# Attention to a few agents ahead of a cosine feed-forward layer: the places of side work move from steps 1, 3 and 5 of a chunk to 2, 4 and 6

## The chip, the cores and the metric

The kernel runs on one core of a Trainium2 chip. The metric is the device time of one execution in microseconds; the lower, the better. The engines are TensorE (PE; its weight loads are listed apart as PEld), VectorE (DVE), ScalarE (ACT), GpSimd (POOL) and SyncE (SP), whose queue issues the DMAs.

## What is computed

Four batches of 12,480 tokens of 128 channels attend to 49 agents: the agents gather values over all keys, each query gathers from the agents, and every token then goes through a feed-forward layer of 2,048 hidden columns with g = h cos(h). All arrays are float32.

```python
def sm(a, b):
    s = scale * (a @ b.transpose(0, 2, 1))
    s = s - s.max(-1, keepdims=True)
    e = np.exp(s)
    return e / (e.sum(-1, keepdims=True) + 1e-09)
a2k = sm(agents, k)
agent_v = a2k @ v
q2a = sm(q, agents)
x = (q2a @ agent_v).reshape(B * N, C)
h = x @ w_in
return (h * np.cos(h)) @ w_out
```

## The kernel before

The agents' values times w_in are one small matrix `a` of 49 rows (held twice) by 2,048 per batch, so a token's hidden columns come straight from its 49 weights: h = a^T pT. A query group of 960 tokens (13 groups a batch, 52 in all) is two chunks of 480 columns; a chunk is NP = 8 steps of two blocks of 128 hidden columns each. The main loop counts steps n over all chunks, 16 to a group. A step issues:

- a hidden pair: two matmuls of 480 columns into a `ph` tile (L557). There are three `ph` buffers of two PSUM banks;
- its cosine on ACT (`c`, L560) and (c - 1) h on DVE (`r`, L562), which frees the `ph` buffer;
- whatever the plan holds for step n (`plan.run(n)`);
- the output pair of the step n - LAG, four steps back: two matmuls into the chunk's output `po` (L579). Step 7 of a chunk adds two more (L575, L576), and then ACT copies `po` to `osb` (L581).

`po` takes one of the two buffers of the pool `ps_1` (`one` in the profile). The side work shares the other: agent scores of the next batch (L90, copied by ACT at L173), query scores (L90, copied at L351; then the maximum on DVE at L355 and a subtraction on POOL), transposes of a group's weights (`query_turned`, L379, copied by ACT at L381; then four POOL operations that make `pT`), values (L235, added by DVE at L240), and projections to the next `a` (L266). A lot of scores, transposes or values fills one buffer of that pool until it is copied.

The plan gives each such lot a step by `extra(n, ...)`: the first step at or after n that no other lot has and whose output step (n - LAG) % 8 is allowed. `dense=True` allows more places; it is used beside a burst. A burst is a stretch on ACT with a table load, exponentials of agent scores and query scores, and a table load back to the cosine, at steps 108, 132 and 156 of a batch (output step 0), and an early one near step 18. The tile scheduler then orders each engine's instructions: it takes what is ready by its own model, in the priority of the code, so a lot may be issued ahead of the step at which the code has it.

In the profile an L90 matmul has two records, so a lot of eight has 16; an L557 or L579 matmul has one.

Of the kernel before, what the change touches and what calls it, by code (L numbers as in the profile page):

```python
# [35 lines left out]
LAG = 4  # L36
# [4 lines left out]
def agent_attention_cos_ffn(ctx, tc, qT, kT, v, agT, w_in, w_out, outT):  # L41
# [9 lines left out]
    NP = NF // 2  # L51
# [250 lines left out]
    with ExitStack() as pools:  # L302
# [152 lines left out]
        taken = set()  # L455

        def extra(n, f, *args, dense=False):


            while n in taken or (n - LAG) % NP not in ((1, 2, 3, 4, 5) if dense else (1, 3, 5)):  # L460
                n += 1
            taken.add(n)
            plan(n, f, *args)
            return n

        for n in range(1, NQ):
            plan(n * STEP - 10, query_weights, n)
            extra(n * STEP - 7, query_turned, n)

        def spread_out(todo, t, end):  # L470

            for i, lot in enumerate(todo):
                t = extra(t, *lot) + 1
                if i + 1 < len(todo):
                    t += max(0, (end - t) // (len(todo) - i - 1) - 1)
            return t
# [9 lines left out]
        def beside(at, todo):  # L486

            for lot in todo[:3]:
                extra(at, *lot, dense=True)
            return todo[3:]  # L490
# [236 lines left out]
```

## Time and profile before

| | |
|---|---|
| median of 3 runs | 1238.58 us (1237.95 to 2774.02) |
| profiled execution | 1242.72 us |
| its span, first to last instruction | 1241.0 us |
| mean granted TensorE clock | 0.971 |
| PE busy, weight loads busy | 1180.0 us (95%), 975.0 us (79%) |
| DVE busy | 1067.3 us (86%) |
| ACT busy | 982.4 us (79%) |
| POOL busy | 353.5 us (28%) |

The busy time of PE is a sum over records whose ends are modelled; the rows below give starts as well. Times in rows are from the start of the span.

### The profile page before, as it was taken

How to read it: one execution, taken by the hardware profiler on the slowest of the kernel's cores; microseconds unless marked ns; L12 is line 12 of the kernel's file. 1: busy time of each engine (PE TensorE's matmuls, PEld its weight loads, DVE VectorE, ACT ScalarE, POOL GpSimd, SP SyncE). 2: the span in 40 equal slices, each digit the busy share in tenths (PEclk: the TensorE clock that was granted, in tenths of full speed). 3: DMA queues.
4: the chain of work that ended last, by engine and by line, in shares of the span. 5: the costliest groups of instructions: out<-in, count | busy, mean ns of one | idle time of the engine just before them, and what ended most of it. 6: DMA issues, size and time to landing. Idle time of an engine off the chain costs nothing.

```text
span 1241.0 us, 17334 instructions
## 1 busy us (share of the span) xinstructions
PE 1180.0 (95%) x6349; PEld 975.0 (79%) x6349; DVE 1067.3 (86%) x1171; ACT 982.4 (79%) x1176; POOL 353.5 (28%) x389
## 2 busy tenths in 40 slices
PE   8998999899999999989999999998999999998997
PEld 8887888788887888868787888887878776776674
DVE  6797888877889988887989888887888999999997
ACT  2267788878878888778878888887887888888996
POOL 1102313433331313172332313126331323121220
PEclk9798999989999999989999999998999999998999
DMA  8782332124422233322241232332321001000000
GB/s 313 217 229 66 104 103 80 64 69 141 126 80 68 76 96 96 99 63 94 65 128 64 80 98 78 96 96 80 96 80 49 32 32 48 16 33 17 32 32 35
DMA packets 39190, 107.74 MB, mean 87 GB/s; under 512 B 4344, under 2 KB 4728, under 8 KB 39096
## 3 DMA queue, kind: packets, MB, share of 16 engines
q1 hardware_dynamic: 39096, 106.55, 27.4%
q8 instruction: 52, 0.85, 0.3%
q14 instruction: 42, 0.34, 0.1%
HBM read 80.97 MB, written 25.56 MB: 86 GB/s over the span
## 4 chain that ended last, share of the span: by engine, by line
PE 70%; DVE 12%; ACT 12%; issue 4%; DMA 0%; POOL 0%; ACTq 0%; SPq 0%; DVEq 0%
PE ph L557 25%; PE one L579 18%; PE one L90 12%; DVE r L562 9%; ACT c L560 6%; PE one L235 5%; ACT osb L581 3%; PE ph L235 3%; PE one L575 2%; PE one L576 2%; PE one L379 1%; PE ph L98 1%; ACT e L360 1%; DVE mx L355 1%; PE one L266 1%
## 5 line engine op out<-in xcount | busy, mean ns | idle before, releaser
L562 DVE SCALAR_TENSOR_TENSOR r<-c,ph 128x960 fp32r<-128x960 f32 x832 | 924.1, 1149 | 96.2 <-ACT c L560 90.4
L560 ACT ACTIVATE c<-ph 128x960 f32<-128x960 f32 x832 | 797.7, 978 | 166.4 <-PE ph L557 147.6
L557 PE MATMUL ph<-pT,a 113*128 113x480 f32 x1664 | 546.9, 410 | 16.9 <-DVE r L562 14.2
L579 PE MATMUL one<-r,w 128*128 128x480 f32 x1664 | 513.2, 390 | 1.2 <-ACT osb L581 0.7
L557 PEld LDWEIGHTS ph<-pT,a 113*128 113x128 f32 x1664 | 287.4, 192 | 114.5 <-DVE r L562 56.7
L579 PEld LDWEIGHTS one<-r,w 128*128 128x128 f32 x1664 | 310.9, 191 | 47.7 <-ACT osb L581 2.0
L90 PEld LDWEIGHTS one<-ag,xt 128*120 128x120 f32 x1408 | 180.6, 194 | 49.5 <-ACT osb L581 27.9
L90 PE MATMUL one<-ag,xt 128*120 128x49 f32 x1408 | 180.2, 273 | 21.5 <-ACT e L351 10.9
L370 POOL TENSOR_TENSOR p<-e,rz 120x392 f32<-120x392 f32 x52 | 44.3, 857 | 474.2 <-PE one L379 397.2
L385 POOL TENSOR_TENSOR pT<-p,pT 49x480 fp32r<-49x480 f32 x104 | 126.7, 1218 | 8.0
L235 PEld LDWEIGHTS one<-s,vt 120*128 120x128 f32 x624 | 77.8, 191 | 10.2 <-ACT osb L581 4.3
L357 POOL TENSOR_TENSOR e<-e,mx 120x392 f32<-120x392 f32 x49 | 41.3, 844 | 155.7 <-DVE mx L355 150.9
L384 POOL CAST pT<-p 49x480 fp32r<-49x480 f32 x104 | 60.7, 584 | 75.5 <-ACT p L381 53.0
L235 PE MATMUL one<-s,vt 120*128 120x98 f32 x624 | 79.3, 273 | 2.5 <-DVE av L240 1.1
L581 ACT COPY osb<-one 128x480 f32<-128x480 f32 x104 | 57.7, 554 | 3.0 <-PE one L579 2.9
L224 POOL TENSOR_TENSOR es<-es,s 120x392 f32<-120x392 f32 x36 | 36.7, 1020 | 46.5 <-ACT s L216 44.1
L379 PEld LDWEIGHTS one<-ident,p 120*113 120x113 f32 x208 | 31.7, 178 | 12.2 <-ACT osb L581 7.1
L575 PE MATMUL one<-pT,b 113*128 113x480 f32 x104 | 40.5, 389 | 0.0
L212 POOL TENSOR_TENSOR s<-s,mxb 120x1568 f32<-120x1568 f32 (+1 forms) x9 | 31.6, 3537 | 29.8 <-DVE mxb L208 29.8
L576 PE MATMUL one<-pT,b 113*128 113x480 f32 x104 | 39.9, 384 | 0.0
L379 PE MATMUL one<-ident,p 120*113 120x120 f32 x208 | 37.6, 274 | 2.3 <-ACT osb L581 2.3
L351 ACT COPY e<-one 120x392 f32<-120x392 f32 x49 | 23.8, 487 | 18.7 <-PE one L90 18.4
(92 smaller groups left out, 544.1 us busy)
## 6 DMA issues: line engine op xcount, KB each, us to landing
xt<-qT SPq DMA_DIRECT2D x52, 480.0 KB, 3.5
vt<-v SPq DMA_DIRECT2D x104, 240.0 KB, 3.4
outT<-osb SPq DMA_DIRECT2D x51, 480.0 KB, 2.6
xt<-kT SPq DMA_DIRECT2D x46, 480.0 KB, 3.5
c<-kT SPq DMA_DIRECT2D x6, 480.0 KB, 5.6
raw<-w_in SPq DMA_DIRECT2D x8, 256.0 KB, 4.8
raw<-w_out SPq DMA_DIRECT2D x8, 256.0 KB, 4.6
outT<-osb SPq DMA_DIRECT2D x2, 240.0 KB, 2.9
```

Of the source, the lines that this page charges most:

```text
L90: nc.tensor.matmul(ps[:, t, :], xt[:, t * TT:(t + 1) * TT], ag[:, b, :], start=True, stop=True)
L235: nc.tensor.matmul(po, vt[:, t, :], twice(e[:, t, :]), start=(t == 0 and (g == 0 or not lone)), stop=(t == GT - 1 and (g == NG - 1 or not ...
L379: nc.tensor.transpose(pt[:KR, t * TT:(t + 1) * TT], p_in[n % 2][:, t, :KR], ident[:TT, :TT])
L384: nc.gpsimd.tensor_copy(pT[own, c], p[own])
L385: nc.gpsimd.tensor_sub(pT[other, c], p[own], pT[own, c].bitcast(F32))
L557: nc.tensor.matmul(ph[:, j, :CH], ai[:, f], pTs[q % 3][:, c], start=True, stop=True)
L560: nc.scalar.activation(cos, h, AF.Sin, bias=HALF_PI, scale=1.0)
L562: nc.vector.scalar_tensor_tensor(r, cos, 1.0, h, op0=ALU.subtract, op1=ALU.mult)
L575: nc.tensor.matmul(po, b1[k], pTs[q % 3][:, c], start=False, stop=False)
L576: nc.tensor.matmul(po, b2[k], pTs[q % 3][:, c], start=False, stop=False)
L579: nc.tensor.matmul(po, w1[:, f, :], r[:, j, :], start=(f == 0), stop=(f == NF - 1))
L581: nc.scalar.copy(osb[:, c * CH:(c + 1) * CH], po)
```

## The change

The places in which `extra` may put a lot are one output step later: 2, 4 and 6 for 1, 3 and 5, and 2 to 6 for 1 to 5 beside a burst.

```diff
         def extra(n, f, *args, dense=False):


-            while n in taken or (n - LAG) % NP not in ((1, 2, 3, 4, 5) if dense else (1, 3, 5)):
+            while n in taken or (n - LAG) % NP not in ((2, 3, 4, 5, 6) if dense else (2, 4, 6)):
                 n += 1
             taken.add(n)
             plan(n, f, *args)
```

Of 202 lots 173 stand one step later in the plan. The others stand one to five steps earlier: where a lot found place 5 past or taken and went to place 1 of the next chunk, it may now find place 6 free. The early burst follows its last query lot and is at step 17 instead of 18.

PE's order in the main loop, in the first chunk of a query group, from the hidden pair (L557) ahead of the chunk's first output pair (L579). L90, eight in all, is a lot of query scores, L379 the transposes. Before:

```order
L557 MATMUL ph<-pT_87,a_80 128x480 x2
L579 MATMUL one<-r,w_68 128x480 x2
L90 MATMUL one<-ag,xt 120x49 x2
L557 MATMUL ph<-pT_87,a_80 128x480 x2
L90 MATMUL one<-ag,xt 120x49 x6
L579 MATMUL one<-r,w_68 128x480 x2
L557 MATMUL ph<-pT_87,a_80 128x480 x2
L579 MATMUL one<-r,w_68 128x480 x2
L379 MATMUL one<-ident,p_93 113x120 x3
L557 MATMUL ph<-pT_87,a_80 128x480 x2
L579 MATMUL one<-r,w_68 128x480 x2
L379 MATMUL one<-ident,p_93 113x120
```

And now, at the same place:

```order
L557 MATMUL ph<-pT_87,a_80 128x480 x2
L579 MATMUL one<-r,w_68 128x480 x2
L90 MATMUL one<-ag,xt 120x49 x3
L557 MATMUL ph<-pT_87,a_80 128x480 x2
L579 MATMUL one<-r,w_68 128x480 x2
L90 MATMUL one<-ag,xt 120x49 x3
L557 MATMUL ph<-pT_87,a_80 128x480 x2
L90 MATMUL one<-ag,xt 120x49 x2
L579 MATMUL one<-r,w_68 128x480 x2
L557 MATMUL ph<-pT_87,a_80 128x480 x2
L579 MATMUL one<-r,w_68 128x480 x2
L379 MATMUL one<-ident,p_93 113x120 x3
```

The lot begins behind the same output pair in both; its six last matmuls, which stood in one block, are now two parts with an output and a hidden pair between, and the transposes stand one step later.

ACT's order around the same place, from the copy of one finished chunk (osb) to the copy of the next but one; `e` is the query scores' copy, `p` the transposes', `s` that of agent scores. Before:

```order
L581 COPY osb<-one 128x480
L560 ACTIVATE c<-ph 128x960 x2
L351 COPY e<-one 120x392
L560 ACTIVATE c<-ph 128x960 x2
L381 COPY p<-one 113x480
L560 ACTIVATE c<-ph 128x960 x4
L581 COPY osb<-one 128x480
L560 ACTIVATE c<-ph 128x960 x2
L173 COPY s<-one 120x392
L560 ACTIVATE c<-ph 128x960 x4
L173 COPY s<-one 120x392
L560 ACTIVATE c<-ph 128x960 x2
```

And now:

```order
L581 COPY osb<-one 128x480
L560 ACTIVATE c<-ph 128x960 x3
L351 COPY e<-one 120x392
L560 ACTIVATE c<-ph 128x960 x2
L381 COPY p<-one 113x480
L560 ACTIVATE c<-ph 128x960 x3
L581 COPY osb<-one 128x480
L560 ACTIVATE c<-ph 128x960 x3
L173 COPY s<-one 120x392
L560 ACTIVATE c<-ph 128x960 x3
L173 COPY s<-one 120x392
L560 ACTIVATE c<-ph 128x960 x2
```

Three of the four copies of side work stand one cosine later; the osb copies and the last copy stand where they did.

PE's order at the first burst of a batch (step 108), from the last output pair that PE can issue during the burst. Before:

```order
L579 MATMUL one<-r,w_68 128x480 x2
L90 MATMUL one<-ag,xt 120x49 x8
L557 MATMUL ph<-pT_87,a_80 128x480 x2
L90 MATMUL one<-ag,xt 120x49 x8
L557 MATMUL ph<-pT_87,a_80 128x480 x2
L579 MATMUL one<-r,w_68 128x480 x2
L557 MATMUL ph<-pT_87,a_80 128x480 x2
```

And now:

```order
L579 MATMUL one<-r,w_68 128x480 x2
L557 MATMUL ph<-pT_87,a_80 128x480
L90 MATMUL one<-ag,xt 120x49 x8
L557 MATMUL ph<-pT_87,a_80 128x480 x2
L90 MATMUL one<-ag,xt 120x49 x8
L557 MATMUL ph<-pT_87,a_80 128x480
L579 MATMUL one<-r,w_68 128x480 x2
L557 MATMUL ph<-pT_87,a_80 128x480 x2
L90 MATMUL one<-ag,xt 120x49 x8
```

The first matmul of the next hidden pair stands ahead of the score lot that was next, and a third score lot follows where there was none.

## Rows read from the trace of the kernel before

**Rows 1.** The page: the span, and the chain of waits that ended last, by engine.
```profile
span 1241.0 us, 17334 instructions
...
PE 70%; DVE 12%; ACT 12%; issue 4%; DMA 0%; POOL 0%; ACTq 0%; SPq 0%; DVEq 0%
```

**Rows 2.** Who waited for whom over the whole span: engine, tile and line, what it waited for, us in total, times, the longest.
```profile
PEld ph L557 <- DVE r L562: 56.7, 146, 0.8
...
PEld one L90 <- ACT osb L581: 27.9, 45, 3.6
...
PE ph L557 <- DVE r L562: 14.2, 39, 4.3
...
PE one L90 <- ACT e L351: 10.9, 3, 3.6
...
PE ph L98 <- DMA xt<-kT: 5.1, 1, 5.1
```

**Rows 3.** Busy time in two stretches of 16 steps: length, then PE, weight loads, DVE, ACT and POOL (instructions in brackets), the granted clock, DMA share and GB/s. The first has three score lots and one of transposes, the second transposes alone.
```profile
183.58:205.44 21.86, 21.17 (x121) 17.98 (x121) 19.12 (x20) 17.81 (x23) 5.29 (x6) 1.00 0.29 90
...
1147.04:1164.90 17.86, 17.18 (x72) 12.39 (x72) 17.36 (x17) 16.18 (x20) 4.39 (x5) 1.00 0.07 28
```

**Rows 4.** The chain of waits within the first of these stretches, in order of time: start, us, what.
```profile
183.58 0.62 PE one L90 x4
...
184.70 1.20 PE one L90 x12
...
191.32 0.44 PE one L579 x2
...
194.14 0.62 PE one L90 x4
```

**Rows 5.** The timeline of the same place: start, us, engine, line, operation, out<-in and shapes, count, and in brackets the idle time ahead and what ended it.
```profile
183.58 0.49 PEld L90 LDWEIGHTS one<-ag,xt 128*120 128x120 f32 x4 [0.60 <-ACT osb L581]
183.58 0.62 PE L90 MATMUL one<-ag,xt 128*120 128x49 f32 x4 [0.20 <-ACT osb L581]
...
186.24 0.60 PE L557 MATMUL ph<-pT,a 113*128 113x480 f32 x2
...
186.88 0.97 ACT L560 ACTIVATE c<-ph 128x960 f32<-128x960 f32 x1 [0.46 <-PE ph L557]
...
187.88 1.15 DVE L562 SCALAR_TENSOR_TENSOR r<-c,ph 128x960 fp32r<-128x960 f32 x1 [0.99 <-ACT c L560]
...
188.95 0.55 DVE L355 TENSOR_REDUCE mx<-e 120x8 f32<-120x392 f32 x1
...
189.74 0.60 PE L579 MATMUL one<-r,w 128*128 128x480 f32 x2
190.62 0.30 PEld L557 LDWEIGHTS ph<-pT,a 113*128 113x128 f32 x2 [0.69 <-DVE r L562]
190.62 0.70 PE L557 MATMUL ph<-pT,a 113*128 113x480 f32 x2 [0.29 <-DVE r L562]
```

**Rows 6.** The first and the last of the 14 hidden pairs that waited for DVE in this way, one in each 16-step stretch with three score lots.
```profile
149.53 0.70 PE L557 MATMUL ph<-pT,a 113*128 113x480 f32 x2 [0.40 <-DVE r L562]
...
791.39 0.70 PE L557 MATMUL ph<-pT,a 113*128 113x480 f32 x2 [0.29 <-DVE r L562]
```

**Rows 7.** The first bursts of three batches: the timeline on DVE and PE, and busy time in stretches, columns as in rows 3.
```profile
246.10 1.09 DVE L562 SCALAR_TENSOR_TENSOR r<-c,ph 128x960 fp32r<-128x960 f32 x1
...
246.40 3.44 PE L90 MATMUL one<-ag,xt 128*120 128x49 f32 x16 [3.62 <-ACT e L351]
249.62 1.15 PE L557 MATMUL ph<-pT,a 113*128 113x480 f32 x2
...
550.61 2.25 PE L90 MATMUL one<-ag,xt 128*120 128x49 f32 x16 [3.62 <-ACT e L351]
...
848.52 3.11 PE L90 MATMUL one<-ag,xt 128*120 128x49 f32 x16 [3.61 <-ACT e L351]
...
242.80:246.40 3.60, 0.00 (x1) 0.00 (x1) 2.54 (x4) 3.57 (x5) 3.39 (x5) 0.77 0.00 0
246.40:258.40 12.00, 12.00 (x46) 10.92 (x47) 7.65 (x9) 5.57 (x7) 8.06 (x10) 0.50 0.30 82
...
240.00:270.00 30.00, 26.38 (x121) 22.79 (x119) 20.43 (x22) 22.09 (x27) 18.72 (x20) 0.77 0.28 83
540.00:570.00 30.00, 26.18 (x133) 22.79 (x132) 21.06 (x23) 22.62 (x26) 20.12 (x18) 0.83 0.27 82
```

**Rows 8.** The early burst: the first cosine behind it on ACT and the scores that PE issued next.
```profile
111.38 0.97 ACT L560 ACTIVATE c<-ph 128x960 f32<-128x960 f32 x1
...
112.85 3.44 PE L90 MATMUL one<-ag,xt 128*120 128x49 f32 x16 [3.20 <-ACT osb L581]
```

**Rows 9.** The timeline further on in the stretch of rows 5: POOL's last two operations on one group's weights, the first hidden pair that reads them, and the copy of a score lot and what follows it up to the next osb copy.
```profile
191.78 2.52 POOL L385 TENSOR_TENSOR pT<-p,pT 49x480 fp32r<-49x480 f32 x2
...
200.61 0.68 PE L557 MATMUL ph<-pT,a 113*128 113x480 f32 x2
...
202.20 0.48 ACT L173 COPY s<-one 120x392 f32<-120x392 f32 x1
...
203.96 0.98 ACT L560 ACTIVATE c<-ph 128x960 f32<-128x960 f32 x1 [0.35 <-PE ph L557]
...
204.84 0.55 ACT L581 COPY osb<-one 128x480 f32<-128x480 f32 x1
```

## The prediction

> **What bounds the kernel now.** I read the page's chain of waits first: 70% of the span lies on PE, 12% on DVE, 12% on ACT [rows 1]. So I ask what PE waits for. The list of waits [rows 2] names three things inside the long main loop: scores that wait for the copy of a finished output chunk (PE L90 <- ACT osb), hidden matmuls that wait for DVE to free one of the three ph buffers (L557 <- DVE r), and three long waits for a copy of query scores (PE L90 <- ACT e, 10.9 us). That is little, so the question is how much of each the change can reach.
>
> The main loop has two regimes. In one query's 16 steps of the loop with two lots of agent scores, one of query scores and one of transposes, 21.86 us pass, DVE is busy for 19.12 and PE's records cover 21.17; in the last part of the program, where hardly anything but transposes is left beside the steps, 16 steps take 17.86 us and DVE fills 17.36 of them [rows 3]. So PE sets the pace in the first regime and DVE in the second. The change moves scores; it can only tell in the first. The trace holds 14 such 16-step stretches, four before 240 us and five before each of 540 and 840 us.
>
> Inside one, the chain shows the price of each thing on PE [rows 4]: a pair of 480-column matmuls takes 0.44 us, twelve score records 1.20 us, so 0.10 each (each score matmul is two records). Between two waits for osb, from 183.58 to 194.14, PE has 16 score records, 16 pairs, two single 480-column matmuls (L575, L576) and 4 transposes, which I price like score records: 1.6 + 7.04 + 0.44 + 0.4 = 9.5 of 10.56 us. The remaining 1.1 us are two stalls: PE's wait for osb, 0.2 us by the matmul's row and 0.60 by the weight load's, and the hidden pair at 190.62 that waits for DVE, 0.29 and 0.69 [rows 5]. I take the middle, 0.45 for the DVE stall and 0.55 for osb's.
>
> **The change, part by part.** It moves 173 of 202 lots one step later; 29 come one to five steps earlier, since the sixth place is still free where the fifth was past or taken. No instruction is added, so engine work is the same. What counts is the order that PE gets, and there the move is smaller than the line suggests: the scheduler still starts a lot right behind the first output pair of a chunk, and only its end moves. Before: two score matmuls, a hidden pair, then six at once; now 3, 3 and 2, with a hidden and an output pair between.
>
> *The wait for osb stays.* The first scores stand at the same place, and they still need the bank that the osb copy frees; the copy keeps its place among ACT's 16 cosines too. Change: 0.
>
> *The DVE stall shrinks.* Before, the second hidden pair behind the wait came at 186.24, after 16 score records; its cosine had waited 0.46 us for it, and DVE then idled 0.99 us [rows 5]. Now 12 records precede it, so it comes 4 x 0.10 = 0.4 us earlier, and its r with it. The maximum of the query scores (0.55 us on DVE at 188.95) also comes one r later, so the next r gains about 0.6 us, and the pair at 190.62 no longer waits: PE is ready for it at 189.74 + 0.44 = 190.18, and that r would now end near 190.0. What is late next: the two r behind it, which now have the 0.55 us maximum ahead of them; the pair after waits some 0.1 us. And the osb copy behind ACT's cosines takes up a part: if PE is 0.45 us early, the wait for osb grows by about 0.1. I book 0.3 us per stretch, 14 x 0.3 = **-4.2 us**. Bounds: 0 (the osb copy takes it all up) and 14 x 0.69 = -9.7. The stall recurs in all 14, from 149.53 to 791.39 [rows 6].
>
> *The second score lot of a stretch* moves from 3, 3, 2 to 3, 3, 2 with its last part one output pair (0.44 us) later. Its copy on ACT began at 202.20, two cosines before the osb copy at 204.84 [rows 9], and keeps that place; I take 0, with 0.44 us each as the upper bound (first rival).
>
> *The first burst of a batch* (exponentials on ACT at steps 108, 316 and 524). PE runs dry and waits 3.62, 3.62 and 3.61 us for the copy of query scores [rows 7]. Before, a score lot was next; now half a hidden pair (one L557) stands ahead of it, and that needs the r that DVE wrote from 246.10 to 247.19, so PE restarts at 247.2, not 246.40: +0.8, and about 0.1 for handing over. Three times: **+2.7 us**. Bounds: 0 and 3 x 1.15, a half-clock pair's record at 249.62. One more query lot comes into this place and leaves the next chunk: the sum is the same.
>
> *The early burst* (step 18, now 17). PE waited 3.20 us for osb behind ACT's exponentials [rows 8]. One score lot (16 x 0.10 = 1.6 us) now stands ahead of the wait, and its copy is DVE's, which idles there; but the osb copy comes one cosine (0.97) later. Net **-0.6 us**, between -1.6 and +1.0.
>
> *The rest.* Values in the second and third bursts: PE still has four lots to fill the wait; 0. Transposes come up to one step (1.4 us) later, and with them four POOL operations ending at 194.30 (191.78 + 2.52); the first matmul that reads them starts at 200.61 [rows 9]: covered by 6.3 us; without that cover each late microsecond would be PE's. POOL's order is the same. Score loads on SP's queue move with their buffers' release; the only wait for such a load is the first (5.1 us, at the start) [rows 2]: 0. The projections move one cosine later among 16 steps: 0.
>
> *Clock.* After each long wait the granted clock is 0.50, which is 1.2 GHz, for a time: 0.77 over 240 to 270 us but 0.83 over 540 to 570 [rows 7], that is 13.8 and 10.2 us at half clock by (1 - share) / 0.5 x 30. The difference costs up to 3.6 x 0.5 = 1.8 us of PE work per burst and I cannot say which way it falls: 0, bounds +-5.4 for three. The Trainium skill, TensorE: Matmul & The Clock Gate, part 1, says that the throttled clock is the default and that activity lifts it; the trace agrees (0.77 in the wait, 0.50 behind it), and a longer wait would by that rule sooner lengthen than shorten the slow time.
>
> Sum: -4.2 + 2.7 - 0.6 = -2.1 us. The profiled execution took 1242.72 us (span 1241.0 and 1.7 around it), 0.3% above the median of 1238.58; taken off the median, **1236.5 us**.
>
> **Rivals.** *Slower: ACT reaches the osb copy late.* Lots that end one output pair later put their copies behind later cosines and closer to the chunk's end; where the copy still waits when the chunk's last matmul is done, osb and with it the next scores are late by up to 0.44 us. ACT still waits 0.35 us for PE ahead of the cosine at 203.96 [rows 9], so it decides once a copy is more than 0.35 late; the 0.45 us by which PE would be earlier uses that slack up. Twice in 14 stretches: 28 x 0.44 = +12.3, about 1251. Against: the copy's place among the cosines is unchanged.
>
> *The waits for osb go as well*, as they would if a lot really began a step later: 28 x 0.55 + 14 x 0.45 = -21.7, about 1217. Against: the order of PE's rows.
>
> *DVE takes the gain.* With 19.12 of 21.86 us busy DVE may just idle elsewhere and hold the ph buffers as late as before: the -4.2 falls away, about 1240.7. The Trainium skill, Trainium Kernel Development and Optimization, Performance Expectations, calls matmul busy time a bad metric and the weight loads' share a good one: here 17.98 of 21.86, less than DVE, which would make DVE the engine to watch. For PE: the sum of its work above, 9.5 of 10.56 us.
>
> *The slow clock lasts longer* in all three bursts: +5.4, about 1242.
>
> **How the numbers follow.** Forecast 0.47, DVE takes the gain 0.20, late osb copies 0.14, clock 0.11, waits gone 0.08. The likeliest gives 1236.5. Low end: the stalls at their bound and the bursts for nothing, -9.7 - 1.6 = -11.3, 1227. High end: no gain, the bursts and the early one at theirs, 3.45 + 1.0, 1243, and the slow clock in two bursts of three, 3.6 more: 1247. That takes in the DVE and the clock case; it leaves out the late copies in full and the waits gone. A comparison of this kernel tells 2% (25 us) from nothing; no single case gets there, only two together: faster 0.04, same 0.91, slower 0.05.
>
> **What would show it.** In the changed profile: still about 45 weight loads of L90 that wait for osb, some 28 us; fewer than 146 waits of L557's loads for DVE, with the one behind the transposes gone from the 14 stretches; a stretch of 21.5 to 21.6 us instead of 21.86; and in the first bursts a wait of L557 for DVE of 4.4 us in place of L90's 3.62. I am wrong if the osb waits are gone or longer, or if slow clock shows in the second or third burst of a batch.

## The result and the profile after

The changed kernel took 1253.46 us (median of 4 runs, 1253.0 to 1258.32) beside 1238.26 us of the kernel before in the same session (four executions; the ratio leaves out the one of 2774.02 us): a ratio of 1.0116, with a 95% interval of 1.0075 to 1.0158. It is slower by 15 us, less than the 2% bound and outside the range of 1227 to 1247.

The profiled execution took 1253.82 us, its span is 11.0 us longer than that of [rows 1], and the chain has more PE and less DVE in it. From the page of the changed kernel, the span and the chain by engine:

```profile
span 1252.0 us, 17335 instructions
...
PE 74%; ACT 10%; DVE 8%; issue 3%; DMA 3%; POOL 0%; SPq 0%; ACTq 0%; DVEq 0%; POOLq 0%
```

The list of waits, to be read against [rows 2] (engine, tile and line, what it waited for, us in total, times, the longest):

```profile
PEld ph L557 <- DVE r L562: 58.1, 169, 1.2
...
ACT e L351 <- PE one L90: 31.5, 16, 4.1
...
PE ph L557 <- DVE r L562: 29.1, 33, 5.5
...
PEld one L90 <- ACT osb L581: 20.9, 43, 0.6
...
PEld ph L557 <- POOL pT L385: 18.0, 4, 5.9
```

PE's matmuls wait 29.1 us for DVE's r instead of 14.2, in fewer places (33 for 39) but up to 5.5 us long, and the three long waits for ACT's copy of query scores are gone from the list.

**Where the time is.** I put both traces side by side by the start of every osb copy, of which there is one per chunk, 104 in all. Of the 11.0 us longer span, +1.5 come before the first copy (an execution of filler_in_before below, which has the code of before up to there, differs from before by -3.3 in this place, so +1.5 is within chance), -1.9 from the next three chunks (the early burst), -4.8 from the three sections with the 16-step stretches (-1.5, -1.7, -1.7), +14.4 from six chunks, two at each first burst of a batch, and +1.9 from the chunks behind those bursts, which I did not follow further. The windows of two stretches, columns as in [rows 3]; the stretch of before had 21.86 us:

```profile
181.80:203.20 21.40, 21.20 (x121) 17.89 (x121) 19.27 (x19) 17.50 (x24) 5.28 (x6) 1.00 0.30 92
411.63:433.05 21.42, 21.21 (x122) 17.90 (x121) 19.29 (x20) 17.49 (x23) 5.29 (x7) 1.00 0.30 93
```

And the two chunks at the three first bursts, from osb copy to osb copy, before:

```profile
236.72:268.69 31.97, 28.15 (x137) 24.65 (x136) 21.97 (x24) 23.70 (x29) 20.77 (x20) 0.79 0.26 78
540.93:572.06 31.13, 27.31 (x137) 23.77 (x137) 22.02 (x24) 23.81 (x29) 20.73 (x20) 0.84 0.26 79
838.85:870.03 31.18, 27.37 (x137) 23.89 (x136) 22.01 (x24) 23.70 (x29) 20.73 (x20) 0.84 0.27 79
```

and after:

```profile
234.82:270.74 35.92, 30.37 (x138) 26.80 (x138) 23.04 (x24) 23.75 (x28) 21.91 (x21) 0.76 0.23 69
542.19:578.01 35.82, 30.34 (x138) 26.75 (x138) 23.04 (x24) 23.71 (x28) 21.84 (x21) 0.76 0.23 69
843.53:880.43 36.90, 31.40 (x138) 27.61 (x137) 23.30 (x24) 23.92 (x28) 21.86 (x21) 0.72 0.22 67
```

They grew by 3.95, 4.69 and 5.72 us. I had booked 0.9 for each. The granted clock, the last column but two, is lower in all three, over a longer time.

**What stands there.** The timeline of the first of these bursts in the changed kernel, with DVE, POOL and PE:

```profile
231.90 10.51 POOL L212 TENSOR_TENSOR s<-s,mxb 120x1568 f32<-120x1568 f32 x3 [16.53 <-DVE mxb L208]
242.35 1.22 POOL L384 CAST pT<-p 49x480 fp32r<-49x480 f32 x2
243.64 2.46 POOL L385 TENSOR_TENSOR pT<-p,pT 49x480 fp32r<-49x480 f32 x2
243.70 1.17 DVE L365 TENSOR_SCALAR rz<-rz 120x32 f32<-120x32 f32 x1
244.91 0.35 DVE L366 RECIPROCAL rz<-rz 120x32 f32<-120x32 f32 x1
245.18 2.15 DVE L562 SCALAR_TENSOR_TENSOR r<-c,ph 128x960 fp32r<-128x960 f32 x2
246.42 0.74 PE L557 MATMUL ph<-pT,a 113*128 113x480 f32 x1 [5.55 <-DVE r L562]
246.95 3.28 PE L90 MATMUL one<-ag,xt 128*120 128x49 f32 x16
...
256.18 3.28 PE L90 MATMUL one<-ag,xt 128*120 128x49 f32 x16
```

and the same operations before, where the burst's table load on ACT began at 239.48, and not at 237.57 as after:

```profile
232.65 10.52 POOL L212 TENSOR_TENSOR s<-s,mxb 120x1568 f32<-120x1568 f32 x3 [16.51 <-DVE mxb L208]
243.09 1.22 POOL L384 CAST pT<-p 49x480 fp32r<-49x480 f32 x2
244.39 2.48 POOL L385 TENSOR_TENSOR pT<-p,pT 49x480 fp32r<-49x480 f32 x2
...
244.39 1.20 POOL L385 TENSOR_TENSOR pT<-p,pT 49x480 fp32r<-49x480 f32 x1
...
245.61 0.18 DVE L365 TENSOR_SCALAR rz<-rz 120x32 f32<-120x32 f32 x1
```

(The row of 1.20 us is the first of the two L385, taken alone.) PE restarts 246.42 - 237.57 = 8.85 us behind the table load, where it was 246.40 - 239.48 = 6.92. Two things are new. POOL's three shifts of the agent scores (L212) start 1.16 us later against the table load (231.90 is 5.67 ahead of it; 232.65 was 6.83 ahead), since the lot whose maximum they wait for (`mxb`, the plan's `spread`) moved one place on; so the four operations behind them come later too. Before, the first of the two L385 was over when DVE's small addition L365 began (244.39 + 1.20 = 245.59, and 245.61); now it has just begun (243.64, and 243.70). The addition takes 1.17 us, to 244.87; the first L385, 1.19 us alone, ends at 244.83. DVE's r comes behind the addition. And a third score lot stands at 256.18, still at half clock: 3.28 us.

### The profile page after: what moved, and what is told of

It is laid out like the page before. It is cut to its first block, busy times and chain, and to the rows that moved or that the text cites. A ratio compares the mean times of both kernels' runs of the same rounds, so it can differ in the third digit from the quotient of the medians.

```text
span 1252.0 us, 17335 instructions
## 1 busy us (share of the span) xinstructions
PE 1186.2 (95%) x6349; PEld 976.9 (78%) x6349; DVE 1070.6 (86%) x1171; ACT 976.1 (78%) x1176; POOL 355.5 (28%) x389
## 4 chain that ended last, share of the span: by engine, by line
PE 74%; ACT 10%; DVE 8%; issue 3%; DMA 3%; POOL 0%; SPq 0%; ACTq 0%; DVEq 0%; POOLq 0%
PE ph L557 27%; PE one L579 22%; PE one L90 12%; DVE r L562 6%; ACT c L560 6%; PE one L235 5%; ACT osb L581 2%; PE one L379 2%; PE ph L98 2%; PE one L575 2%; PE one L576 2%; DMA vt<-v 1%; PE one L266 1%; ACT e L360 1%; DMA xt<-kT 1%
## 5 line engine op out<-in xcount | busy, mean ns | idle before, releaser
L557 PE MATMUL ph<-pT,a 113*128 113x480 f32 x1664 | 553.6, 414 | 30.8 <-DVE r L562 29.1
L579 PE MATMUL one<-r,w 128*128 128x480 f32 x1664 | 513.0, 391 | 2.1 <-DVE s L171 1.7
L557 PEld LDWEIGHTS ph<-pT,a 113*128 113x128 f32 x1664 | 283.8, 193 | 128.7 <-DVE r L562 58.1
L579 PEld LDWEIGHTS one<-r,w 128*128 128x128 f32 x1664 | 311.6, 192 | 49.4 <-ACT p L381 2.1
L90 PEld LDWEIGHTS one<-ag,xt 128*120 128x120 f32 x1408 | 191.4, 199 | 34.2 <-ACT osb L581 20.9
L90 PE MATMUL one<-ag,xt 128*120 128x49 f32 x1408 | 188.2, 276 | 4.2 <-ACT osb L581 4.0
L385 POOL TENSOR_TENSOR pT<-p,pT 49x480 fp32r<-49x480 f32 x104 | 126.4, 1215 | 8.0
L384 POOL CAST pT<-p 49x480 fp32r<-49x480 f32 x104 | 60.7, 584 | 75.7 <-ACT p L381 49.3
L379 PEld LDWEIGHTS one<-ident,p 120*113 120x113 f32 x208 | 30.9, 176 | 15.4 <-ACT osb L581 10.1
L379 PE MATMUL one<-ident,p 120*113 120x120 f32 x208 | 38.1, 274 | 4.0 <-ACT osb L581 4.0
L355 DVE TENSOR_REDUCE mx<-e 120x8 f32<-120x392 f32 x49 | 27.2, 555 | 16.6 <-ACT e L351 12.6
```

Of the source, the lines that this page charges most:

```text
L90: nc.tensor.matmul(ps[:, t, :], xt[:, t * TT:(t + 1) * TT], ag[:, b, :], start=True, stop=True)
L379: nc.tensor.transpose(pt[:KR, t * TT:(t + 1) * TT], p_in[n % 2][:, t, :KR], ident[:TT, :TT])
L384: nc.gpsimd.tensor_copy(pT[own, c], p[own])
L385: nc.gpsimd.tensor_sub(pT[other, c], p[own], pT[own, c].bitcast(F32))
L557: nc.tensor.matmul(ph[:, j, :CH], ai[:, f], pTs[q % 3][:, c], start=True, stop=True)
L579: nc.tensor.matmul(po, w1[:, f, :], r[:, j, :], start=(f == 0), stop=(f == NF - 1))
```

## The experiments

Three causes of the 14.4 us were in question: the order at the restart (half a hidden pair ahead of the scores, my +0.9), the late shifts, and the third score lot; behind all of them the slow clock. Each kernel's "loss" below is the sum over the two chunks at the three first bursts against the trace of before, and "slow" is the time at a granted clock of 0.50 there, from the trace's clock records. A bracket in the column of waits names a second wait further on. The kernel before took 1240.2 us beside burst_queries_back, dense_places_only, shifts_early and no_third_lot, 1238.4 beside third_lot_alone, filler_in_before, filler_in_after and filler_and_burst_back, and 1243.0 beside no_eps_add, burst_all_back and burst_back_filler_9.

Loss and slow time are read from one execution of each kernel, and executions differ. The 81 of the kernel before that ran beside these took 1234.7 to 1248.5 us, at mean granted clocks of 0.982 to 0.968; by (1 - clock) / 0.5 x span that is 44 to 80 us of slow time in the whole program, and the longer ones have more of it. So two rows that differ by one or two us of loss, or by 3 to 7 of slow time, may differ by chance, and the measured ratios are the check. The four executions of the changed kernel had 0.960 to 0.968, which is 80 to 100 us.

| kernel | wait at restart, us | third lot | slow, us | loss, us |
|---|---|---|---|---|
| before | 3.62 | no | 34.1 | 0 |
| after | 5.5 | yes | 54.6 | 14.4 |
| burst_queries_back | 3.62 | no | 34.1 | 0.2 |
| third_lot_alone | 3.62 | yes | 44.4 | 5.0 |
| dense_places_only | 4.53 | no | 41.0 | 4.1 |
| no_third_lot | 5.5 | no | 44.4 | 7.6 |
| no_eps_add | 4.53 | yes | 51.2 | 11.4 |
| shifts_early | 4.54 | yes | 58.0 | 12.2 |
| burst_all_back | 3.63 | no | 30.7 | -0.8 |
| filler_in_before | 0.6 (1.8 later) | no | 23.9 | 2.1 |
| filler_in_after | 0.8 | yes | 0 | -7.2 |
| filler_and_burst_back | 0.6 (1.75 later) | no | 6.8 | -5.6 |
| burst_back_filler_9 | none (1.7 later) | no | 0 | -8.6 |

**burst_queries_back**: the query scores beside the first burst at the old places, and the lot behind it in the next chunk again; all else changed.

```diff
-                    todo = beside(at, scored(ps[2]) if b > 1 else scored(ps[1]))
+                    todo = beside(at, scored(ps[2]) if b > 1 else scored(ps[1]), True)
...
-                t = spread_out(todo, t, o + BURSTS[min(k + 1, 2)] - 4)
+                t = spread_out(todo, t + 3 * (k == 0), o + BURSTS[min(k + 1, 2)] - 4)
```

(`True` hands the old places 1 to 5 down to `extra`.)

> The changed kernel, with only the query scores beside the first burst of a batch back at their old places (1 to 5, and the fourth lot in the next chunk); all else stays one place later. Theory A (the loss is made at the first bursts by PE's order there: half a hidden pair ahead of the score lot, and a third lot in the slow clock): the three bursts lose nothing, the 14 stretches keep their 0.44 us each, so about 1232 us, 1228 to 1237. Rival B (the loss comes from POOL: the agents' shifts start one step later, so pT and DVE's r behind the burst are late whatever PE does): the bursts still lose about 2 us each and the longer slow clock, 1243 to 1250.

Measured: 1238.08 us, ratio 0.9969 (0.9944 to 0.9994), just above what Theory A said; the loss is 0.2 us, and the three sections keep their -1.5, -1.6 and -1.7. What is lost at the first bursts can be undone alone, without giving up the gain of the stretches.

The shifts are as late in this kernel as in the changed one, and DVE's addition is as slow (1.17, 1.22 and 1.20 us):

```profile
236.16 1.17 DVE L365 TENSOR_SCALAR rz<-rz 120x32 f32<-120x32 f32 x1
237.63 1.09 DVE L562 SCALAR_TENSOR_TENSOR r<-c,ph 128x960 fp32r<-128x960 f32 x1
```

But PE restarted with its score lot at 236.95, ahead of this r, after the old wait of 3.63 us. So the late shifts cost nothing under the old order; they count only where half a hidden pair, which needs r, stands first.

**dense_places_only**: the changed places beside bursts, the old ones elsewhere.

```diff
-not in ((2, 3, 4, 5, 6) if dense else (2, 4, 6)):
+not in ((2, 3, 4, 5, 6) if dense else (1, 3, 5)):
```

> The kernel before with only the places beside a burst moved (2 to 6); scores, transposes and POOL's shifts elsewhere stay at 1, 3 and 5. PE's order at the first burst has half a hidden pair ahead of the score lot, as in the changed kernel, but no third lot and no late shifts. Theory A: PE restarts behind DVE's r instead of the copy, 0.9 us later in each first burst, and the slow clock may last longer: 1241 to 1248 us. Rival B (POOL's late shifts): no loss, 1236 to 1240. Rival C (the third lot in the slow clock): no loss either, 1236 to 1241.

Measured: 1248.23 us, ratio 1.0052 (1.0023 to 1.0081), at the upper end of Theory A. PE's restart:

```profile
241.18 0.74 PE L557 MATMUL ph<-pT,a 113*128 113x480 f32 x1 [4.56 <-DVE r L562]
```

The shifts are in time here (L365 takes 0.18 us), there is no third lot, and the wait is 0.9 us longer than before. That is the term I had forecast for the order; its price in time is 4.1 us in three bursts rather than 2.7, since the slow time grows by 6.9 us.

**shifts_early**: the changed kernel with the shifts' lots at their old places.

```diff
-            t = extra(t, ab[b].across)
-            t = extra(t + 1, ab[b].spread)
+            t = extra(t - 1, ab[b].across, early=True)
+            t = extra(t + 1, ab[b].spread, early=True)
```

> The changed kernel with only the two lots ahead of POOL's shifts (the agents' maximum turned and spread) at their old places, so that the shifts and with them pT are one step earlier; PE's order behind the first burst stays the changed one. Rival B: PE's wait falls from 5.5 us to about 4.4 in the three first bursts, and the slow clock with it: 1243 to 1248 us. Theory A in its strict form (PE's order alone): 1251 to 1254 us.

Measured: 1247.9 us, ratio 1.0055 (1.0032 to 1.0077); waits of 4.57, 4.52 and 4.52 us. The late shifts hold PE by 1.0 us a burst. The slow time, which was expected to fall too, did not in this trace (58.0 us).

**no_third_lot**: the changed kernel with the lot behind the first burst in the next chunk again (the second line pair of burst_queries_back alone).

> The changed kernel with the fourth query lot beside the first burst kept out of that chunk (it goes to place 2 of the next one); the order ahead of it and the shifts stay as changed. Rival C (the third lot runs at half clock and holds up the steps, 3.3 us for 1.7): 3 x 1.7 and up to 3 us of slow clock per burst less, 1243 to 1248 us. If the restart alone makes the loss: 1251 to 1254 us.

Measured: 1244.56 us, ratio 1.0030 (1.0000 to 1.0059); the waits stay at 5.5, the loss falls from 14.4 to 7.6 us. The lot is the largest single piece, by the loss and by the ratio, although its work is done anyway, a chunk later: the two chunks hold 64 score records in every kernel of the table.

**third_lot_alone**: the first line pair of burst_queries_back alone, so that the order up to the restart is the old one and only the third lot is left.

> The changed kernel with three of the four query lots beside the first burst back at their old places, so that PE's order up to the restart is the old one, but the fourth lot still in that chunk, at place 6. If the third lot in the slow clock costs by itself, the bursts lose 1 to 2.3 us each against the run with all four lots back (which lost nothing): 3 to 7 us, a ratio to before of 0.999 to 1.003. If it costs only together with the late restart: ratio 0.996 to 0.998, as with all four back.

Measured: 1242.54 us, ratio 1.0006 (0.9969 to 1.0043); loss 2.4, 2.7 and -0.1 us. In the first two bursts the slow time is 17.1 us, in the third 10.2 as before, and there the lot costs nothing (31.12 us for the two chunks, 31.18 before). So the lot costs through the clock, and the clock did not answer it in the same way each time. The ratio is where it was expected for a lot that costs by itself.

**no_eps_add**: the changed kernel without DVE's L365.

```diff
-            nc.vector.tensor_scalar_add(rz, rz, EPS)
             nc.vector.reciprocal(rz, rz)
```

> The changed kernel without the addition of the constant 1e-9 to the sums of the query weights (DVE L365), so that part of the computation is left out. In the changed kernel that addition took 1.17 us at the first burst, until the first of POOL's two L385 was done, where it took 0.18 before the change. Theory A (the whole shift chain on POOL is late, and reaches PE by two roads, through DVE's r and through pT itself, which is done at 246.10 against 246.26 for r): with the addition gone only the r is early, PE then waits for pT, and the wait at the first bursts is still 5.3 to 5.5 us; time ratio to the changed kernel's 1.0116 unchanged within 0.3%. Theory B (the slowed small operation on DVE is the cause by itself): the wait is 4.4 to 4.6 us. Theory C (the reciprocal that stands behind it takes the delay over): L366 takes over 1 us instead of 0.35, and the wait stays at 5.5.

Measured: 1245.54 us, ratio 1.0037 (1.0007 to 1.0068). The restart (lines from 365 on are numbered one lower here):

```profile
239.05 2.47 POOL L384 TENSOR_TENSOR pT<-p,pT 49x480 fp32r<-49x480 f32 x2
239.09 0.35 DVE L365 RECIPROCAL rz<-rz 120x32 f32<-120x32 f32 x1
239.49 2.22 DVE L561 SCALAR_TENSOR_TENSOR r<-c,ph 128x960 fp32r<-128x960 f32 x2
240.75 0.19 PEld L556 LDWEIGHTS ph<-pT,a 113*128 113x128 f32 x1 [4.90 <-POOL pT L384]
240.79 0.61 PE L556 MATMUL ph<-pT,a 113*128 113x480 f32 x1 [4.53 <-DVE r L561]
```

Theory B. My own theory A was wrong: PE starts at 240.79 although POOL's two L384 run to 241.52. The pair reads pT of the group's first chunk, which the first of them writes, and that one is over at 240.24 (1.19 us by its own row); the view names it for the weight load. DVE's r, over at 240.64, is what came last. So the second road of theory A is there, but 0.4 us ahead of the first. The reciprocal and r run beside the same POOL operation at their usual 0.35 and 1.1 us: the slowed addition alone made the last 1.0 us of the wait. (The time fell by more than the 3.0 us of the loss. In its trace 2.6 us of that lie at the early burst, where 3.4 us are slow instead of 10.2; burst_queries_back, whose edit does not reach the early burst, has the same there, so I take it for chance.)

**filler_in_before**: the kernel before, with a hidden pair repeated 7 times at step 111 of the first three batches, so that PE has work in the burst. The repeats write the same numbers again.

```diff
+                if n % PER == BURSTS[0] + 3 and n < (NB - 1) * PER:
+                    for _ in range(7):
+                        for j in range(2):
+                            f = slice((2 * i + j) * P, (2 * i + j + 1) * P)
+                            nc.tensor.matmul(ph[:, j, :CH], ai[:, f], pTs[q % 3][:, c], start=True, stop=True)
                 h = ph[:, :, :CH]
```

> The kernel before; at the first burst of the three batches PE repeats the hidden pair of the third step behind the burst seven times (same operands, same ph buffer, same result) ahead of the next output pair, 3.1 us of the 3.6 it idles. Nothing else moves. Theory A2 (a good part of a first burst's cost is the slow clock that follows PE's wait): slow time after these bursts falls from 34 us towards 0 and the time by 8 to 15 us, ratio 0.988 to 0.994. If the slow clock costs little because PE waits there anyhow: ratio 0.998 to 1.002.

Measured: 1238.40 us, ratio 0.9994 (0.9965 to 1.0023): a miss. The ratio is that of the other case, in which the slow clock costs little, but the trace doesn't decide for it, since the slow time fell only from 34.1 to 23.9 us. The wait at the restart is down from 3.6 to 0.6 us and the scores run at full clock, but PE meets another one 3 us on (lines from 562 on are numbered five higher here):

```profile
246.52 2.46 POOL L357 TENSOR_TENSOR e<-e,mx 120x392 f32<-120x392 f32 x3
247.41 0.56 DVE L355 TENSOR_REDUCE mx<-e 120x8 f32<-120x392 f32 x1 [2.76 <-POOL e L357]
247.89 2.21 DVE L567 SCALAR_TENSOR_TENSOR r<-c,ph 128x960 fp32r<-128x960 f32 x2
249.09 0.70 PE L557 MATMUL ph<-pT,a 113*128 113x480 f32 x2 [1.80 <-DVE r L567]
```

A maximum waits on DVE for POOL, the r queue behind it, PE waits 1.80 us, and slow clock begins at 250.8 (6.8, 6.8 and 10.2 us in the three bursts), 19.9 us behind the osb copy ahead of the burst, where it began 8.0 us behind it in the kernel before.

**filler_in_after**: the changed kernel with 11 repeats.

> The changed kernel with the same filler, eleven repeats for its longer wait of 5.5 us. Theory A2: the slow time falls from some 55 us towards 0, and of the 14.4 us that the three bursts lose against before only the later restart is left (3 x 1.9 us), beside the gain of the 14 stretches; ratio to before 0.985 to 0.995. If the restart is the whole loss: ratio 1.007 to 1.012.

Measured: 1233.65 us, ratio 0.9952 (0.9925 to 0.9979), at the upper edge of what was expected. The two chunks at the three first bursts:

```profile
234.19:263.24 29.05, 28.05 (x160) 23.84 (x160) 22.85 (x24) 23.48 (x28) 24.00 (x22) 1.00 0.28 85
534.72:563.69 28.97, 28.10 (x160) 23.82 (x160) 22.83 (x24) 23.52 (x29) 23.91 (x22) 1.00 0.27 85
829.25:858.26 29.01, 28.11 (x160) 23.83 (x159) 22.86 (x24) 23.51 (x29) 23.96 (x22) 1.00 0.28 85
```

22 more matmuls in each, and each is 6.9 to 7.9 us shorter than in the changed kernel: 21.6 us in all, more than the whole loss. Late addition and third lot are still there; at full clock, with PE's wait filled (0.83 us of it is left), they cost little that shows: the six chunks are 1.35 us longer than in burst_back_filler_9, which has neither.

**filler_and_burst_back**: the old order at the first bursts (as burst_queries_back and shifts_early together) with 7 repeats.

> The changed kernel with the query scores beside the first burst and the two lots ahead of POOL's shifts at their old places, and the filler of seven repeats. Sum of the single gains: 14 x 0.44 and 8 to 15 us of slow clock off the kernel before: ratio 0.981 to 0.990.

Measured: 1228.62 us, ratio 0.9914 (0.9889 to 0.9939), a little above what was expected, faster than both kernels. The trace is of the longest of its ten executions (1236.28 us). At the first bursts slow clock is left in it only in the third, 6.8 us behind a wait of 1.75 us.

**burst_all_back**: the same without the repeats.

> The changed places everywhere but at the first burst of a batch: query scores beside it, shifts ahead of it and the fourth query lot behind it stand as in the kernel before. Nothing is added. If the loss is in the first bursts alone, and the gain of the 14 stretches (0.44 us each) is kept: waits of 3.6 us for ACT's copy, about 34 us of slow clock there, the time 4 to 7 us below the kernel before, ratio 0.994 to 0.997. If the two are tied together (the stretches gain only because the fourth lot left them): ratio 0.999 to 1.002.

Measured: 1240.65 us, ratio 0.9987 (0.9957 to 1.0017). The time alone doesn't tell the two cases apart; the trace does: the bursts are at -0.8, -0.0 and -0.0 us against before and the sections at -1.3, -1.5 and -1.6. The gain of the stretches shows in every trace that has the changed places there, but is too small to show in this comparison.

**burst_back_filler_9**: filler_and_burst_back with 9 repeats.

> The same with 9 instead of 7 repeats of a hidden pair for PE in the first bursts (4.0 us of filling for a wait of 3.6). With 7 repeats slow clock was left in the third burst alone, 6.8 us behind a second wait of 1.75 us for DVE. If the filling decides: no slow clock at all there, ratio 0.987 to 0.991. If the second wait decides: 6 to 14 us of slow clock are left in one or more of the three, and the ratio is 0.991 to 0.994 since PE is also held 0.4 us longer.

Measured: 1228.12 us, ratio 0.9883 (0.9823 to 0.9943; four executions), where it was expected if the filling decides, and not to be told from filler_and_burst_back. The two chunks at the first bursts:

```profile
235.36:263.98 28.62, 26.67 (x154) 22.73 (x153) 21.54 (x24) 23.56 (x29) 20.86 (x20) 1.00 0.29 87
535.54:564.08 28.54, 26.66 (x155) 22.74 (x155) 21.61 (x24) 23.56 (x29) 20.81 (x20) 1.00 0.29 87
829.66:858.18 28.52, 26.62 (x155) 22.71 (x154) 21.60 (x24) 23.56 (x28) 20.79 (x20) 1.00 0.29 87
```

No slow clock, although the second wait (1.70 to 1.76 us) is still there in all three. That this second wait went with slow clock in all three bursts of filler_in_before, in one of filler_and_burst_back and in none here stays open.

## Why the prediction was wrong

**Right.** *The osb wait stays*: 43 weight loads, 20.9 us, where I had said about 45 and 28 (the one of 3.6 us, at the early burst, is gone). *The DVE stall shrinks*: 11 of the 14 stretches are shorter by 0.41 to 0.45 us, three by 0.07 to 0.22, the sections together by 4.8 where the sum had 4.2; the pair behind the transposes waits no longer, and the stretch of 21.40 us is a little below the 21.5 to 21.6 I named. That also answers the rival in which DVE takes the gain: DVE fills 19.27 of 21.40 us and gave the time back. The late osb copies didn't come, and the waits for osb didn't go; that the rival with the late copies names about 1251, close to what was measured, is luck. *The second score lot*: nothing to be seen. *The early burst*: -1.9 for -0.6, the sign right, but beyond its bound of -1.6; PE waits 1.72 us there, for DVE's copy s, which I had taken for free, where it had waited 3.20 for osb [rows 8]. Five more kernels with the changed places and, as here, 10.2 us of slow clock in that place have -1.7 to -2.4. One sign that I named came out the other way: 169 waits of L557's loads for DVE, not fewer than 146, and 58.1 us for 56.7. In the stretches one load that waited 0.69 or 0.70 us mostly became two that wait some 0.26 and 0.33 (at 190.32 and 191.38 us in the changed trace): the stall shrank, but moved on to the two pairs behind, where I had said that one would wait some 0.1.

**Wrong: the first burst, +2.7 for 14.4 measured.** Three steps failed.

- *"PE restarts at 247.2, not 246.40: +0.8, and about 0.1 for handing over."* By itself this was right: dense_places_only, shifts_early and no_eps_add have waits of 4.51 to 4.57 us, 0.9 more. But it took DVE's r from the trace of before as it stood. Another part of the change, the shifts one place later, put POOL's L385 beside the addition that stands ahead of this r on DVE, which then took 1.17 us for 0.18, and the wait was 5.5. I had followed the moved POOL operations only to their reader ("covered by 6.3 us") and had noted that POOL's order is the same; what runs beside them on another engine I had not asked. Price: 3.0 us in the traces, from 14.4 to the 11.4 of no_eps_add.
- *"One more query lot comes into this place and leaves the next chunk: the sum is the same."* In the place it comes into, PE runs at half clock: 3.28 us for the lot against 1.81 at full clock (16 records at 109.44 us in the changed trace). And the slow time goes on longer with it. Price: 6.8 us in the traces by no_third_lot, 5.0 by third_lot_alone.
- *"The difference costs up to 1.8 us of PE work per burst and I cannot say which way it falls: 0."* It fell one way in all three: 17.1, 17.1 and 20.5 us of slow clock for 13.7, 10.2 and 10.2.

These prices are those of one edit at a time, and they don't add up. By the ratios each edit alone gives back more than its trace says: from 1.0116 the time falls to 1.0030 without the third lot, to 1.0037 without the addition and to 1.0055 with the early shifts, some 11, 10 and 8 us, more together than was lost, the last with an interval that touches the changed kernel's. That the new places of the query scores beside the first bursts are the cause is shown by burst_queries_back; how the loss divides among restart, addition, lot and clock is not.

The windows of [rows 7] in the changed kernel, and one more behind the third:

```profile
240.00:270.00 30.00, 24.45 (x105) 21.75 (x104) 18.72 (x20) 18.19 (x23) 16.06 (x18) 0.72 0.25 81
540.00:570.00 30.00, 24.52 (x111) 21.70 (x110) 18.29 (x20) 18.39 (x21) 21.66 (x17) 0.72 0.23 66
840.00:870.00 30.00, 24.50 (x114) 21.67 (x113) 19.20 (x21) 18.89 (x23) 22.21 (x17) 0.72 0.20 54
870.00:900.00 30.00, 29.54 (x158) 25.14 (x156) 22.70 (x22) 25.68 (x29) 8.83 (x11) 0.94 0.25 89
```

By the working of the prediction, (1 - share) / 0.5 x 30, these are three times 16.8 us of slow clock and 3.6 more behind the third, 54.0, where before had 13.8 + 10.2 and, over 840 to 870 at 0.83, another 10.2: 34.2. The clock records give 54.6 and 34.1. Half of the 20.5 us is work that PE didn't do, 10.2 us; with three restarts 1.93, 1.86 and 1.87 us later, 5.7, that makes 15.9 for 14.4 measured. The half is an upper bound. Nine bursts have the wait of 3.6 us and no third lot (before, burst_queries_back, burst_all_back): the seven with 10.2 us of slow clock take 31.12 to 31.18 us for the two chunks, the two with 13.7 take 31.97 and 32.25, so 3.4 us of slow clock cost 0.8 to 1.1 there; by that estimate 20.5 us cost 5 to 7. So the clock is at least about as large a part as the later restarts, perhaps the larger, and of the mechanisms named the rival "the slow clock lasts longer in all three bursts" was the nearest, at 1242, but too small: it had bounded the term by the difference between two bursts of the same kernel, which says nothing of what a longer wait and more work behind it bring.

**The range** was too narrow for the same reason: its high end let the slow clock grow in two bursts and the restart by 1.15 us each, and both went beyond that.

## What to carry to other kernels

When an edit moves work, ask for each moved operation not only who reads its result but what will now run beside it: a small operation on the path to a restart can become six times as long. Where PE runs dry for microseconds, look at the granted clock behind it before counting what a moved lot costs, since work put there runs at half speed and the sum over two chunks is not the same. And a wait that can't be removed may be worth filling with repeated matmuls: 18 to 22 of them in each of three places took 8 to 22 us off the chunks around them here, all three places together (burst_back_filler_9 against burst_all_back, filler_in_after against the changed kernel). In the kernel before, 14 of them in each place gained nothing (filler_in_before): PE ran into a wait of 1.8 us further on, and 23.9 of 34.1 us of slow clock stayed.

## What the runs showed of the hardware

DVE's addition to a 120x32 tile (a tensor_scalar, SBUF to SBUF) took 0.18 us at the first bursts before and 1.17, 1.18 and 1.19 us after, in each case until POOL's tensor operation on SBUF that had started before it was done; a reciprocal of the same tile beside the same operation took 0.35 us with or without it, and r, which reads one operand from PSUM, 1.1. The Trainium skill, SBUF — State Buffer, Who interferes with whom, says that a tensor_scalar can take the port pair that the two engines share, and that whoever issues first has it for its whole instruction while the other is blocked; the trace agrees, the 1.17 us ending with POOL's first L385 (244.87 and 244.83).

The slow time behind a wait was not a fixed price in these runs. Behind the same wait of 3.6 us it was 10.2 or 13.7 us without a third lot and 10.2 or 17.1 with one; behind 4.5 us it was 13.7 without and 17.1 or 20.5 with it; behind 5.5 us 13.7 or 17.1 without and 17.1 or 20.5 with it. What decides within these I can't tell from the rows.
